# One load of w1 in place of two: the third and fourth column run in packets of 2048 B

## The chip, the core and the metric

The kernel runs on one core of one Trainium2 chip. The metric is the device time of one execution in microseconds. Times in the profile count from the start of the span, the profiled part of one execution.

## The reference

The input is x of 2048 positions by 448 channels in bfloat16. It is normalised (layernorm), and the result xn feeds two branches, whose product is added to x:

```
xn = layernorm(x)
# branch A: a diagonal complex state-space model, 448 states
h[t] = Lam_bar * h[t-1] + B_bar @ xn[t]
s    = 2 * Re(C @ h) + xn * Dskip
# branch B: an MLP, 448 -> 1792 -> 448
y    = layernorm(xn)
g    = silu(gelu(y @ w1 + b1) @ w2 + b2)
out  = x + s * g
```

w1 has 448 rows and 1792 columns, w2 has 1792 rows and 448 columns, both in bfloat16. A row of w1 is 3584 B.

## The kernel before

The 2048 positions are worked in four groups (0 to 3) of 512, each of two blocks of 128 partitions by two positions of different parity. For a group the kernel computes layernorm, transposes the normalised rows (group 0's first layernorm for the MLP by TensorE at L460, the others by DMA on SP), multiplies by w1 (L809), applies gelu (ScalarE, L813), multiplies by w2 (L836), and beside it runs the state-space branch: L737 makes the input of the scan, L761 scans, L879 to L885 make the output.

**The order.** Each operation is added to a plan as a task with the keys that it reads and writes. `ORDER` is a fixed list of task numbers, which is the order of emission on all engines, and `SECOND` is the list of tasks that take their second engine where two are given. Nothing is rearranged when the program is built. From the keys the plan works out the semaphore waits; every DMA has a semaphore of its own. An instruction that waits holds up everything behind it on its engine.

**w1 in SBUF.** w1 has 448 = 384 + 64 rows. The first 384 rows lie as three row blocks of 128 partitions (slots 0 to 2 of `w1_sb`), the last 64 rows on partitions 64 to 127 of slot 3. The matmul of L809 works with halves of 64 partitions at a time, so two of the eight 64-row pieces have to be on the other half of the partitions than the transfer puts them; for one of them a copy inside SBUF (L354, on VectorE) does this: from partitions 64 to 127 of slot 2 to partitions 0 to 63 of slot 3.

**Runs of columns.** The 14 column tiles of 128 are grouped in four runs, `CH` of L344: run 0 has tiles 0 and 1, run 1 tiles 2 to 5, run 2 tiles 6 to 9, run 3 tiles 10 to 13. `ldw1` (L347) loads the runs that it is given: one transfer of 384 rows, one of 64 rows, and then a copy for each run. A row of runs 1 to 3 has 512 columns, 1024 B; a run 0 row has 512 B.

```
CH = ((0, 2), (2, 4), (6, 4), (10, 4))
def ldw1(cs, prio):
    a, w = CH[cs[0]][0] * 128, sum(CH[c][1] for c in cs) * 128
    ld("sp", w1_sb[:, 0:3, a:a + w], ..., [f"w1_{c}" for c in cs], 384 * w * 2, prio, dur=0.55)
    ld("sp", w1_sb[64:128, 3, a:a + w], ..., [f"w1r_{c}" for c in cs], 64 * w * 2, prio)
    for c in cs:
        ...  # the copy within SBUF of run c: reads w1_{c}, writes w1c_{c}
```

**Who waits for w1.** In `mm1_run` (L792) the matmuls of two column tiles come in two phases. The first phase (6 matmuls) waits for both transfers of its run (`w1_c`, `w1r_c`); the second (8 matmuls) waits for the copy too (`w1c_c`). After them comes gelu on ScalarE, which frees the two PSUM banks. In group 0 the pieces are taken up in this order on TensorE: runs 1 and 0 for block 0, then block 1's transposes (L460), then run 2 for block 0, then run 3 for both blocks together, the first matmuls 512 wide; the rest of block 1 follows.

**SP's queue.** SP issues nearly all transfers, in this order: x of blocks 0 and 1, w1 run 1, run 0, run 2, run 3 (two transfers each), x of blocks 2 and 3, w2 in four parts, then B and C of the state-space branch, and from 19.86 us on the DMA transposes.

**VectorE's order around 10 us.** L453 (the layernorm of block 1), L354 (copy of run 2), two L632 (a table of angles), two L419 (block 1's transposes from PSUM to `xn2T`), L354 (copy of run 3), L561, L632, then L401 (statistics of group 1's layernorm).

Of the kernel before, what the change touches and what calls it, by code (L numbers as in the profile page):

```python
# [155 lines left out]
def dram_ap(t, offset, ap):  # L156
    return bass.AP(tensor=t.tensor, offset=offset, ap=ap)
# [2 lines left out]


ORDER = [int(k) for k in """
1 14 20 0 48 10 17 19 21 15 2 95 27 18 96 92 28 93 22 16 25 49 5 97 13 109 94 91 110 98 105 104 26 106 100 23 99 50 51 56 6 52 66 107 3 111 101 112 57
30 108 29 31 102 113 53 115 24 55 33 54 132 58 118 129 32 119 114 122 171 116 34 47 133 169 134 130 40 131 35 67 172 254 251 103 120 156 41 124 252
253 256 255 170 59 117 121 123 4 9 173 44 127 42 125 128 135 141 257 137 126 136 143 60 138 61 258 139 11 142 43 68 144 162 140 148 146 147 176 163 63
8 72 152 39 38 145 205 158 149 151 207 65 36 165 206 154 166 37 259 177 260 164 277 150 155 261 263 62 264 153 262 70 278 179 175 265 168 279 64 174
178 272 273 274 218 71 73 7 283 193 167 191 45 180 217 194 181 182 75 69 275 192 284 76 195 183 276 280 196 287 215 197 199 281 216 285 160 74 184 291
289 288 282 46 198 286 208 85 187 200 209 250 295 210 211 292 89 201 77 78 86 80 203 249 219 204 214 223 224 227 185 202 213 228 231 221 222 188 225
190 226 229 370 79 81 83 266 82 84 290 294 296 293 300 298 230 304 297 87 299 305 212 374 159 368 367 303 301 324 88 302 306 90 325 232 326 307 220
269 270 327 372 271 308 233 186 234 334 472 267 371 369 373 328 268 235 237 238 335 341 342 339 346 343 329 236 312 239 157 340 330 309 382 375 12 241  # L170
331 383 379 384 365 242 245 376 377 332 380 333 336 240 385 243 386 347 348 189 344 316 337 345 387 350 244 338 247 388 361 313 246 310 349 362 389
356 366 352 363 161 320 311 353 364 471 248 314 381 357 358 351 391 359 378 410 414 412 411 360 447 404 473 476 413 418 354 390 419 392 415 416 317
474 475 393 355 417 477 423 421 422 420 394 427 315 478 450 479 397 424 426 395 428 431 432 425 396 400 401 318 448 321 429 434 435 436 430 433 453
451 398 480 406 439 319 449 399 469 483 402 457 440 484 405 407 441 452 408 454 442 409 510 443 481 482 486 470 511 437 512 513 487 489 403 438 505
514 455 485 444 515 490 518 445 494 516 502 322 519 456 517 488 495 520 523 521 446 461 497 506 538 503 539 522 498 507 540 496 541 543 524 542 462
323 544 545 546 491 492 548 547 549 550 552 551 493 499 458 525 526 508 533 534 504 463 464 527 528 535 536 500 554 532 555 557 529 465 459 556 537
572 553 596 460 466 573 574 467 597 599 530 531 575 598 600 601 602 603 576 558 577 580 581 604 509 605 501 582 560 586 561 578 579 563 566 585 607
588 468 583 564 559 592 590 584 606 587 589 591 569 593 594 595 617 562 565 608 614 609 610 611 570 571 567 618 619 612 615 620 616 621 568 622 613
630 623 631 624 632 625 633 626 627 628 629
""".split()]  # L180
SECOND = [int(k) for k in """
46 54 55 62 64 67 70 75 77 84 108 113 131 134 159 161 163 164 166 178 185 186 188 190 191 221 223 225 227 229 231 239 249 250 259 267 269 332 363 365
366 385 401 402 437 448 469 481 483 488 492 500 502 503 505 511 529 530 610 613
""".split()]


# [14 lines left out]
def bass_recurrent_scan__ssm_conv_s5__mixer_channel_mlp__prompt_kernel(  # L201
# [18 lines left out]
    with ExitStack() as es:  # L220
# [85 lines left out]
        with nc.Block():  # L306
# [26 lines left out]
            def ld(eng, o, i, writes, nbytes, prio, reads=(), dur=0.45):  # L333
                kb.dma(eng, o, i, reads=reads, writes=writes, prio=prio, nbytes=nbytes, dur=dur)
# [4 lines left out]
            def ldx(b0, n, prio, reads=(), eng="sp"):  # L339
                ld(eng, x_all[:, b0:b0 + n, :, :], dram_ap(A_x, b0 * 256 * D, [[2 * D, 128], [256 * D, n], [D, 2], [1, D]]),  # L340
                   [f"x{b}" for b in range(b0, b0 + n)], n * 256 * D * 2, prio, reads, dur=0.25 + 0.2 * n)
# [5 lines left out]
            def ldw1(cs, prio):  # L347
                a, w = CH[cs[0]][0] * 128, sum(CH[c][1] for c in cs) * 128
                ld("sp", w1_sb[:, 0:3, a:a + w], dram_ap(B_w1, a, [[F, 128], [128 * F, 3], [1, w]]), [f"w1_{c}" for c in cs], 384 * w * 2, prio, dur=0.55)
                ld("sp", w1_sb[64:128, 3, a:a + w], dram_ap(B_w1, 384 * F + a, [[F, 64], [1, w]]), [f"w1r_{c}" for c in cs], 64 * w * 2, prio)  # L350
                for c in cs:
                    a, w = CH[c][0] * 128, CH[c][1] * 128
                    low, high = w1_sb[0:64, 3, a:a + w], w1_sb[64:128, 2, a:a + w]
                    kb.either(("dve", lambda e, low=low, high=high: e.tensor_copy(low, high)), ("act", lambda e, low=low, high=high: e.activation(low, high, ACT.Copy)), [f"w1_{c}"], [f"w1c_{c}"])  # L354

            LW = ((0,), (1,), (2,), (3,))

            S1 = 10 * PINNED
            for par in range(0 if 0 else 2):
# [1 line left out]
            ldx(1, 1, S1 + 2)  # L361
            ldw1(LW[0], S1 + 1)
            ld("pool", brows[0:3, :], dram_ap(B_b1, 256, [[512, 3], [1, 512]]), ["br0"], 3072, 0, reads=["br"])
            ld("pool", brows[3:4, 0:256], dram_ap(B_b1, 0, [[256, 1], [1, 256]]), ["br1"], 512, 0, reads=["br"])
            for cs in LW[1:]:
                ldw1(cs, S1 + 3)
# [662 lines left out]
```

## Time and profile before

| | |
|---|---|
| median of 3 runs | 153.82 us (153.58 to 154.24) |
| profiled execution | 153.63 us |
| its span | 151.9 us |
| TensorE, matmuls | 147.6 us busy (97%) |
| VectorE | 128.2 us busy (84%) |
| ScalarE | 98.4 us busy (65%) |
| GpSimd | 40.8 us busy (27%) |
| DMA | 14.73 MB, 31236 packets |

The page of the profile names engines by short names: PE is TensorE, PEld its weight loads, DVE VectorE, ACT ScalarE, POOL GpSimd, SP SyncE. An engine with a q behind its name is the queue of that engine. A row of a timeline has the start, the length, the engine, the line of the kernel, the operation, what it writes and reads, the count, and in brackets the idle time before it with what ended it. The tiles of w1 and w2 are both shown as `w_sb`, the rows of normalised x as `xn_sb`.

### The profile page before, as it was taken

What the parts mean: (1) busy time and instruction counts of PE and PEld (TensorE: products, weight loads), DVE (VectorE), ACT (ScalarE), POOL (GpSimd) and SP (SyncE); (2) the same over time, 40 slices, a digit from 0 to 9 for tenths busy, and PEclk for the clock granted to TensorE, in tenths of its full rate; (3) what the DMA queues carried; (4) which work ended last, traced back from release to release, by engine and by line L of the source; (5) the groups of instructions that cost most, each with busy time, mean ns of one, the idle gap of its engine ahead of it and who ended that gap; (6) DMA issues with size and microseconds to landing.
All of it is one profiled execution on the core that took longest, in us unless ns stands there. A gap on an engine that the chain in (4) does not pass through costs nothing.

```text
span 151.9 us, 2990 instructions
## 1 busy us (share of the span) xinstructions
PE 147.6 (97%) x1136; PEld 87.5 (58%) x1136; DVE 128.2 (84%) x270; ACT 98.4 (65%) x182; POOL 40.8 (27%) x100
## 2 busy tenths in 40 slices
PE   7999999999999999999999999999999999999992
PEld 7886755444566577545444556754444666555561
DVE  3978969899998969999999996379968727999984
ACT  3787998888789559997798610462579833067400
POOL 5377870053021910010366006200071040000200
PEclk9999999999999999999999999999999999999999
DMA  4999999889996100700003032610340001100022
GB/s 117 270 309 389 262 231 182 175 150 154 214 213 165 23 0 0 138 0 4 0 0 63 4 60 53 146 60 4 60 109 14 4 0 60 60 0 0 4 102 79
DMA packets 31236, 14.73 MB, mean 97 GB/s; under 512 B 24752, under 2 KB 30774, under 8 KB 31222
## 3 DMA queue, kind: packets, MB, share of 16 engines
q1 hardware_dynamic: 30912, 14.26, 41.9%
q0 software_dynamic: 160, 0.23, 0.6%
q8 instruction: 9, 0.15, 0.4%
q10 hardware_dynamic: 150, 0.05, 0.1%
q14 instruction: 5, 0.04, 0.1%
HBM read 6.89 MB, written 1.84 MB: 57 GB/s over the span
## 4 chain that ended last, share of the span: by engine, by line
PE 96%; DVE 2%; issue 0%; DVEq 0%
PE psum L809 29%; PE psum L836 28%; PE psum L737 14%; PE psum L879 12%; PE psum L882 4%; PE psum L422 3%; PE psum L720 3%; PE psum L885 1%; DVE t L893 1%; PE psum L460 1%; DVE tmp L899 1%; PE psum L705 1%; PE psum L602 0%; DVE ones L309 0%; PE psum L529 0%
## 5 line engine op out<-in xcount | busy, mean ns | idle before, releaser
L809 PE MATMUL psum<-xn2T,w_sb 64*128 64x512 bf16 (+1 forms) x462 | 44.6, 345 | 0.2
L836 PE MATMUL psum<-w_sb,gT 128*128 128x448 bf16 x224 | 44.4, 353 | 0.0
L813 ACT ACTIVATE gT<-psum,b1f 128x512 bf16<-128x512 f32 (+1 forms) x66 | 36.0, 625 | 10.6 <-PE psum L809 10.4
L809 PEld LDWEIGHTS psum<-xn2T,w_sb 64*128 64x128 bf16 x462 | 24.0, 109 | 19.7 <-ACT gT L813 2.3
L836 PEld LDWEIGHTS psum<-w_sb,gT 128*128 128x128 bf16 x224 | 21.6, 98 | 20.3 <-issue 0.6
L419 ACT ACTIVATE u_sb<-psum 128x512 bf16<-128x512 f32 (+2 forms) x22 | 10.5, 478 | 23.0 <-PE psum L737 22.7
L737 PE MATMUL psum<-xnT,BT 128*128 128x256 bf16 x196 | 24.0, 273 | 0.0
L737 PEld LDWEIGHTS psum<-xnT,BT 128*128 128x128 bf16 x196 | 18.9, 98 | 5.4 <-issue 1.1
L761 DVE TENSOR_TENSOR_SCAN s_w<-dk,vs 128x774 f32<-128x774 f32 x8 | 14.0, 1760 | 0.1
L899 POOL TENSOR_TENSOR tmp<-t,x_all 128x448 bf16<-128x448 bf16 x5 | 5.2, 1031 | 33.1 <-DVE t L896 30.7
L500 ACT ACTIVATE xn_sb<-x_all,lnw 128x448 bf16<-128x448 bf16 (+2 forms) x21 | 13.0, 661 | 1.2 <-DVE xn_sb L499 1.1
L419 ACT ACTIVATE vs<-s_w 64x256 bf16<-64x256 f32 (+2 forms) x16 | 10.9, 682 | 2.6 <-DVE s_w L761 1.5
L879 PE MATMUL psum<-CZ,h_sb 128*128 128x448 bf16 x56 | 11.9, 353 | 0.0
L839 DVE TENSOR_TENSOR o<-psum,b2bc 128x448 f32<-128x448 f32 x16 | 9.7, 614 | 1.7 <-PE psum L836 1.5
L879 PE MATMUL psum<-CQ,h_sb 128*128 128x448 bf16 (+2 forms) x54 | 10.5, 332 | 0.0
L879 PEld LDWEIGHTS psum<-CZ,h_sb 128*128 128x128 bf16 x56 | 5.4, 98 | 4.7 <-DVE lnmv L407 0.4
L401 DVE BATCH_NORM_STATS2 lnst<-x_all 128x6 f32<-128x448 bf16 x12 | 7.0, 614 | 0.6 <-DMA x_all<-in_A_x_dram 0.6
L879 PEld LDWEIGHTS psum<-CQ,h_sb 128*128 128x128 bf16 x54 | 5.1, 98 | 4.0 <-DVE t L893 0.4
L882 PE MATMUL psum<-M,xnT 128*128 128x448 bf16 x32 | 7.4, 352 | 0.0
L891 DVE TENSOR_TENSOR Cr<-psum,xd 128x448 f32<-128x448 f32 x7 | 4.3, 620 | 3.5 <-PE psum L885 3.4
L480 POOL TENSOR_TENSOR lnw<-lnw,mhalf 128x8 f32<-128x8 f32 x3 | 7.0, 2332 | 0.3
L499 DVE TENSOR_SCALAR xn_sb<-x_all,lnw 128x448 bf16<-128x448 bf16 (+2 forms) x19 | 6.9, 395 | 0.0
(160 smaller groups left out, 189.8 us busy)
## 6 DMA issues: line engine op xcount, KB each, us to landing
out_dram<-tmp SPq DMA_DIRECT2D x7, 224.0 KB, 2.0
x_all<-in_A_x_dram SPq DMA_DIRECT2D x3, 448.0 KB, 4.3
w_sb<-in_B_w_dram SPq DMA_DIRECT2D x3, 448.0 KB, 8.5
w_sb<-in_B_w_dram SPq DMA_DIRECT2D x3, 384.0 KB, 4.9
vs<-in_A_C_re_dram SPq DMA_DIRECT2D x1, 392.0 KB, 11.5
Bn<-in_A_B_im_dram SPq DMA_DIRECT2D x1, 336.0 KB, 10.4
Bn<-in_A_B_re_dram SPq DMA_DIRECT2D x1, 336.0 KB, 10.8
vs<-in_A_C_im_dram SPq DMA_DIRECT2D x1, 336.0 KB, 11.3
```

Source lines behind the costliest of these rows:

```text
L401: dve([lambda e, b=b, par=par, q=q: e.bn_stats(lnst[:, q, :], x_all[:, 2 * g + b, par, :])], [f"x{2 * g + b}"] , [f"st{q}"], 0.62, prio)
L419: kb.either(("act", [lambda e, o=o, i=i: e.activation(o, i, ACT.Copy) for o, i in pairs]), ("dve", [lambda e, o=o, i=i: e.tensor_copy(o, i ...
L480: power = fns + [lambda e: e.tensor_tensor(w(2), w(0), mhalf[:].to_broadcast([128, 2, nq]), ALU.pow), lambda e: e.tensor_tensor(w(3), mean ...
L500: ("act", [lambda e, o=o, i=i: e.activation(o, i, ACT.Identity, bias=nb, scale=rs) for o, i in parts], 0.75, 0.2)]
L737: fns = [lambda e, r=r, m=m, d=d: e.matmul(psum[:, 4, r * NK:(r + 1) * NK], BT[:, m, d, :], xnT[:, gx, d, :], start=(d == 0), stop=(d == 6 ...
L761: dve(lambda e, so=so, vi=vi: e.tensor_tensor_scan(so, dk[:].rearrange("p i c -> p (i c)"), vi, 0.0, ALU.mult, ALU.add), ["v", "vl", "dk", ...
L809: return lambda e: e.matmul(view(bk[k]), w1_sb[rows, d, fcol(2 * j + k)], rhs[rows, d, :, :], start=not second and n == 0, stop=second and ...
L813: act([lambda e, k=k: e.activation(gT[:, gb, 2 * j + k, :].rearrange("p (r c) -> p r c", r=2)[:, :, cols], view(bk[k]), ACT.Gelu_apprx_tan ...
L836: fns = [lambda e, fi=fi: e.matmul(psum[:, bk, 0:D], gT[:, gb, fi, q * 128:(q + 1) * 128], w2_sb[:, fi, :], start=(fi == 0), stop=(fi == N ...
L839: dve(lambda e: e.tensor_tensor(o2[:, fb, :], psum[:, bk, 0:D], b2bc[:], ALU.add), [f"ps{bk}", "b2bc"], [f"oo{fb}"], 0.62, prio - 76)
L879: fns = [lambda e, k=k: e.matmul(psum[:, bk, c0:c1], h_sb[:, hb, k, k0:k0 + 128], cm[:, k, c0:c1], start=(k == 0), stop=False) for k in ra ...
L882: fns += [lambda e, d=d: e.matmul(psum[:, bk, c0:c1], xnT[:, gx, d, xs], M0[:, d, c0:c1], start=False, stop=(d == 3)) for d in range(4)]
```

## The change

Runs 2 and 3 go to `ldw1` in one call. There is then one transfer of 384 rows by 1024 columns (768 KB) and one of 64 rows by 1024 columns (128 KB), where there were two transfers of 384 KB and two of 64 KB. A row of it is 2048 B in place of 1024 B. The two copies within SBUF stay as they are; both now depend on the transfer of 384 rows. The tasks have new numbers because there are two fewer, so `ORDER` and `SECOND` are renumbered; the order of all other tasks is as before. SP's queue holds the two new transfers where the first two of the four were.

```diff
-            LW = ((0,), (1,), (2,), (3,))
+            LW = ((0,), (1,), (2, 3))
...
             ldw1(LW[0], S1 + 1)
...
             for cs in LW[1:]:
                 ldw1(cs, S1 + 3)
```

## The prediction

> **What bounds the kernel now.** I read the page first: busy times, then the slices, then the chain of waits.
>
> ```profile
> PE 147.6 (97%) x1136; PEld 87.5 (58%) x1136; DVE 128.2 (84%) x270; ACT 98.4 (65%) x182; POOL 40.8 (27%) x100
> PEclk9999999999999999999999999999999999999999
> DMA  4999999889996100700003032610340001100022
> PE 96%; DVE 2%; issue 0%; DVEq 0%
> ```
>
> TensorE is busy for 97% of the span and 96% of the chain that ended last is its matmuls, one after the other, at a granted clock near full throughout. So the end of the kernel moves by what TensorE is held up, almost one for one, and by nothing else. The DMA engines are full from about 4 to 46 us (a slice is 3.8 us; the first four to six slices hold the loads). The change touches only loads of w1, so the question is whether TensorE comes to wait for one of them.
>
> The timelines of TensorE, of its weight loads and of VectorE around 10 us show where w1 is taken up:
>
> ```profile
> 9.58 0.62 PE L460 MATMUL psum<-ident,xn_sb 128*128 128x128 bf16 x8
> 10.14 1.51 PE L809 MATMUL psum<-xn2T,w_sb 64*128 64x256 bf16 x22
> ```
>
> ```profile
> 10.13 0.25 PEld L809 LDWEIGHTS psum<-xn2T,w_sb 64*128 64x128 bf16 x6
> 10.58 1.35 PEld L809 LDWEIGHTS psum<-xn2T,w_sb 64*128 64x128 bf16 x26 [0.20 <-ACT gT L813]
> ```
>
> ```profile
> 9.31 0.31 DVE L354 COPY w_sb<-w_sb 64x512 bf16<-64x512 bf16 x1 [0.88 <-DMA w_sb<-in_B_w_dram]
> 9.66 0.62 DVE L632 TENSOR_SCALAR s_w<-dk,cw 128x256 f32<-128x256 f32 x2
> 10.19 0.75 DVE L419 COPY xn2T<-psum 128x512 bf16<-128x512 bf16 x2
> 10.97 0.29 DVE L354 COPY w_sb<-w_sb 64x512 bf16<-64x512 bf16 x1
> 12.15 0.63 DVE L401 BATCH_NORM_STATS2 lnst<-x_all 128x6 f32<-128x448 bf16 x1 [0.44 <-DMA x_all<-in_A_x_dram]
> ```
>
> The matmuls at 10.14 are the first that read run 2 of w1 (the program's third run, columns of tiles 6 to 9). They wait for both its transfers, the 384 rows and the 64 rows. VectorE's copy at 9.31 waits for the 384 rows alone, and its idle time of 0.88 us ends with that landing. The queue of transfers says when each landed (answers for windows that hold one issue; KB, then us from issue to landing; issues begin at 4.44, 5.07, 5.61 and 6.24):
>
> ```profile
> w_sb<-in_B_w_dram SPq DMA_DIRECT2D x1, 384.0 KB, 4.9
> w_sb<-in_B_w_dram SPq DMA_DIRECT2D x1, 64.0 KB, 4.5
> w_sb<-in_B_w_dram SPq DMA_DIRECT2D x1, 384.0 KB, 5.2
> w_sb<-in_B_w_dram SPq DMA_DIRECT2D x1, 64.0 KB, 4.8
> ```
>
> So run 2 is complete at 5.07 + 4.46 = 9.53 (the 384 rows at 9.29), and run 3 at 6.24 + 4.78 = 11.02 (its 384 rows at 10.77). TensorE needs run 2 at 10.14, 0.6 us after it lands, and run 3 only with the first 512-wide matmul, at 11.81, 0.8 us after. Both are covered today, by little.
>
> **The change, part by part.** Compared instruction by instruction, every engine but SP keeps its order; SP's four issues become two, in the same place. So the change does what it says; what else can move is time.
>
> 1. *The wait that it adds.* Run 2 no longer lands by itself: everything that wants run 2 waits for run 3 too. At the present rate the last 64 rows would be in at 11.02 as now, since the queue holds the same bytes behind the same predecessors and the DMA engines are full (next table).
>
> 2. *The packets.* 896 packets of 1024 B become 448 of 2048 B. No row has this size, so I bound its rate by the stretches around it (columns: stretch, length, busy of PE, PEld, DVE, ACT, POOL, clock, DMA share, GB/s):
>
> ```profile
> 6.90:8.60 1.70, 1.65 (x32) 1.53 (x33) 1.48 (x8) 1.55 (x3) 0.39 (x1) 1.00 0.98 315
> 8.60:10.10 1.50, 1.50 (x28) 1.22 (x24) 0.76 (x3) 1.25 (x4) 1.21 (x3) 1.00 1.05 270
> 10.10:11.60 1.50, 1.50 (x27) 1.27 (x27) 1.44 (x6) 1.18 (x5) 1.33 (x3) 1.00 1.01 330
> 11.60:12.30 0.70, 0.70 (x14) 0.45 (x9) 0.26 (x2) 0.70 (x2) 0.62 (x3) 1.00 1.02 369
> 12.30:13.50 1.20, 1.20 (x18) 0.66 (x16) 1.20 (x3) 0.95 (x4) 0.54 (x4) 1.00 1.00 387
> ```
>
> Runs 2 and 3 hold 917,504 B and fill the engines from 6.9 to about 10.1; (1.70 x 315 + 1.50 x 270) / 3.2 = 294 GB/s, or 3.12 us. After 10.1 come x, in packets of 1792 B, and w2, mostly in packets of 3584 B. At 330 GB/s the two runs take 2.78 us, 0.34 less; at 369, 0.63 less; at 387, 0.75 less; at the present rate nothing less. I take 330: the stretch after 10.1 is the one nearest in packet size that is not mostly 3584 B. The ends are 0 and 0.75. A loss below zero I keep for a rival. The last rows then land at 11.02 - 0.34 = 10.68, between 10.27 and 11.02. That last landing is the slowest of the DMA engines, and I leave its lag behind the mean as it is.
>
> 3. *TensorE.* The copy at 9.31 began 0.02 after its landing, so the matmuls of 10.14 would begin at 10.70: 0.56 later. Of that, 0.10 is given back at once: the next run of matmuls started at 10.59 because it waited for ScalarE's gelu (the 0.20 of the weight loads above), while its predecessors, at 0.11 us a pair, would have let it go at 10.49. Net +0.46, between 0.05 and 0.80. After that ScalarE's gelu waits for matmuls and the matmuls for gelu, both shifted alike; I find no stretch of TensorE idle time up to 147 us that a DMA or another unshifted thing ends, so the 0.46 reaches the end.
>
> 4. *VectorE behind the added wait.* The first L354 copy waits for the merged 384 rows. They lose the 64 rows that went between (0.24 in landing) and gain most of the 0.34: 10.77 - 0.24 - 0.3 = 10.2. Queued behind it are two L632 (0.62), the two L419 that move block 1's transposes into xn2T, and the other L354. They move by 0.94, so xn2T is ready at 10.94 + 0.94 = 11.9. The 512-wide matmuls need it at 11.81 + 0.46 = 12.27: covered by 0.4. The margin holds if the merged load is later still, since the matmuls wait for the 64 rows behind it. The second copy ends at 12.2 and is needed a microsecond later still. Then L401 is 0.94 - 0.44 = 0.5 late, and with it the layernorm of group 1 and its DMA transposes on SP (issued 19.86 and 21.87, landing 5.4 us later, 27.3; wanted at 30.0). VectorE's next wait for TensorE, 1.20 us before L839 at 22.26, takes up the rest. Cost: nothing, with 0.4 and over 2 us of cover.
>
> 5. *SP.* Two issues fewer (0.50 and 0.59 us, with gaps 1.17): x, w2 and the rest are issued 1.17 earlier. In a full queue this moves their landing only by the 0.3 saved. w2 lands last at 18.5 against 19.3 when it is wanted. Gain: nothing. GpSimd's load of b2, which waits for run 3's 64 rows, is issued at 13.58, long after them.
>
> Sum: +0.46. The profiled execution took 153.63 us (span 151.9, and 1.7 around it), 0.19 under the median of 153.82; the median moves to 154.28, say 154.3. About 0.5%, 0.77 us, is what a measurement of this kernel can tell from no change; the forecast lies inside that.
>
> **Rivals.** *Larger transfer, free of charge* (10%): if packets of 2048 B run like those of 3584 B, at 387 GB/s and more, 0.75 to 0.9 us is saved, the rows are in by 10.1 to 10.3, and TensorE is held by 0.05 or nothing: 153.8 to 153.9. For it: the rate rises steadily in the table. Against it: from 6.9 to 10.1 packets also suffer long latencies that are not a matter of size. The Trainium skill, "DMA: Bandwidth & Descriptors", sections "Anatomy of one DMA" and "Bandwidth", speaks for this rival: it fits a load as 2.0 us plus bytes over 436 GB/s (for GpSimd's queue) and advises batching to 1 MiB. By that, an estimate, the 768 KB would land 3.8 us after issue, at 8.2, and cost nothing; but it gives 2.9 us for the 384 KB that took 4.9 here, so the trace does not bear it out in a full queue.
>
> *The slowest engine decides* (35%): a merged load is complete when the last DMA engine is. Net cost passes 0.77 if the start of the matmuls passes 11.01, which is when the last rows land no earlier than they do now. This happens if the larger packets bring no rate, or if an engine lags. For it: w2's first load, issued at 7.41, took 6.8 us, to 14.2, while x before it was in by 12.2, though its 224 KB need 0.6 us at 369 GB/s: 1.4 us of lag; a fetch of instructions (16 KB) sat on an engine just then. Today such a lag under run 3 has 0.8 us of cover, and after the change none. Price: no rate gained, 154.6; with 1.0 us of lag, 10.68 + 1.0, start at 11.70, net +1.46, 155.3. Against it: the stretch before 10 us shows no such fetch.
>
> *Faster* (7%): the earlier issue pulls in something that TensorE waits for. The trace lists 1.6 us of idle time before weight loads from 9.5 to 20, but ended by ScalarE, by TensorE itself or by issue, not by a DMA. It would give 153.0 at best.
>
> **How the numbers follow.** The forecast, a net cost from 0.1 to 0.77, has 48%. Same: forecast 48% and the free transfer 10%, 58%. Slower: 35%. Faster: 7%. The range goes from 153.6 (the free transfer, less the scatter of the runs before) to 155.1 (a lag of 0.8 us) and leaves out the faster case and the largest lags.
>
> **What would show it.** Right: L809's matmuls of run 2 begin at 10.5 to 11.0 instead of 10.14, with TensorE idle behind the L460 transposes; VectorE's idle time before L354 grows from 0.88 to about 1.9; the later pieces of the chain are shifted by one constant. Wrong: no idle time there (free transfer), matmuls after 11.0 (slowest engine), a second new wait at the 512-wide matmuls for xn2T, or a shift that is not constant after 20 us.

## The result and the profile after

The changed kernel takes 154.93 us in the median (154.83 to 155.79), the kernel before 153.82. The ratio is 1.0088, with a 95% interval of 1.006 to 1.0116: slower by about 1.4 us by the ratio, 1.1 by the medians. The ratios, here and below, leave out slow runs, those that took over 1.5% longer than the fastest of the same kernel; f1_after, f2_join and f4_alone have such runs. The forecast of 154.3, inside the bound of 0.5%, was wrong; the rival of the slowest DMA engine, with 154.6 to 155.3, was right. The stated range, up to 155.1, still holds the 154.93, but on that rival's side of the bound.

The execution whose trace is kept took 155.79 us, one of the two longest. Its span is 2.1 us longer than the one of before, so sizes read from it stand above those of a median run. The page's lines for TensorE, the clock, the DMA engines and the chain of waits:

```profile
PE 147.9 (96%) x1136; PEld 88.0 (57%) x1136; DVE 127.9 (83%) x270; ACT 98.4 (64%) x182; POOL 40.3 (26%) x100
PEclk9999999999999999999999999999999999999999
DMA  4999999989996300510003030801322001200022
PE 89%; DMA 5%; SPq 2%; DVE 1%; issue 1%; DVEq 0%
```

TensorE has the same work (147.9 us against 147.6), but the chain now runs through a load: 7.18 us of it, from 4.42 to 11.60, is the transfer of w1. The timelines of TensorE, its weight loads and VectorE at the same place as before:

```profile
9.95 0.62 PE L460 MATMUL psum<-ident,xn_sb 128*128 128x128 bf16 x8
12.32 2.95 PE L809 MATMUL psum<-xn2T,w_sb 64*128 64x256 bf16 x42 [1.75 <-DMA w_sb<-in_B_w_dram]
```

```profile
12.29 1.94 PEld L809 LDWEIGHTS psum<-xn2T,w_sb 64*128 64x128 bf16 x34 [1.89 <-DMA w_sb<-in_B_w_dram]
```

```profile
11.62 0.29 DVE L354 COPY w_sb<-w_sb 64x512 bf16<-64x512 bf16 x1 [2.81 <-DMA w_sb<-in_B_w_dram]
11.94 0.62 DVE L632 TENSOR_SCALAR s_w<-dk,cw 128x256 f32<-128x256 f32 x2
12.48 0.74 DVE L419 COPY xn2T<-psum 128x512 bf16<-128x512 bf16 x2
13.25 0.29 DVE L354 COPY w_sb<-w_sb 64x512 bf16<-64x512 bf16 x1
```

Run 2's matmuls begin at 12.32 instead of 10.14, after 1.75 us of idle time that the load ends. No 0.20 us of waiting for ScalarE follows. From there every piece of the chain is shifted by one constant: the first product with w2 from 19.39 to 21.46 (2.07), the last output matmuls from 145.43 to 147.51 (2.08). The landings (issued at 4.42 and 5.04):

```profile
w_sb<-in_B_w_dram SPq DMA_DIRECT2D x1, 768.0 KB, 7.2
w_sb<-in_B_w_dram SPq DMA_DIRECT2D x1, 128.0 KB, 7.2
```

The last 64 rows are in at 12.23 (5.04 + 7.19), where run 3's were in at 11.02. A landing is the last of 16 marks, one by each DMA engine. The fastest engine finished the 64 rows at 9.22, before at 9.54; the slowest is 3.0 us behind it, before 1.5.

### The profile page after: what moved, and what is told of

Its sections match the earlier page's. It is cut to its first block, busy times and chain, and to the rows that moved or that the text cites. A ratio compares the mean times of both kernels' runs of the same rounds, so it can differ in the third digit from the quotient of the medians.

```text
span 154.0 us, 2987 instructions
## 1 busy us (share of the span) xinstructions
PE 147.9 (96%) x1136; PEld 88.0 (57%) x1136; DVE 127.9 (83%) x270; ACT 98.4 (64%) x182; POOL 40.3 (26%) x100
## 4 chain that ended last, share of the span: by engine, by line
PE 89%; DMA 5%; SPq 2%; DVE 1%; issue 1%; DVEq 0%
PE psum L836 28%; PE psum L809 27%; PE psum L737 14%; PE psum L879 12%; DMA w_sb<-in_B_w_dram 5%; PE psum L882 4%; PE psum L720 3%; SPq L84 2%; PE psum L885 1%; DVE t L893 1%; DVE tmp L899 1%; PE psum L705 1%; DVEq L138 0%
## 5 line engine op out<-in xcount | busy, mean ns | idle before, releaser
L809 PE MATMUL psum<-xn2T,w_sb 64*128 64x512 bf16 (+1 forms) x462 | 44.5, 345 | 1.9 <-DMA w_sb<-in_B_w_dram 1.7
L809 PEld LDWEIGHTS psum<-xn2T,w_sb 64*128 64x128 bf16 x462 | 24.1, 109 | 21.3 <-ACT gT L813 2.1
L419 ACT ACTIVATE u_sb<-psum 128x512 bf16<-128x512 f32 (+2 forms) x22 | 10.5, 478 | 23.0 <-PE psum L737 22.7
L879 PE MATMUL psum<-CQ,h_sb 128*128 128x448 bf16 (+2 forms) x54 | 10.5, 332 | 0.0
```

What stands on the lines that cost most here:

```text
L419: kb.either(("act", [lambda e, o=o, i=i: e.activation(o, i, ACT.Copy) for o, i in pairs]), ("dve", [lambda e, o=o, i=i: e.tensor_copy(o, i ...
L809: return lambda e: e.matmul(view(bk[k]), w1_sb[rows, d, fcol(2 * j + k)], rhs[rows, d, :, :], start=not second and n == 0, stop=second and ...
L879: fns = [lambda e, k=k: e.matmul(psum[:, bk, c0:c1], h_sb[:, hb, k, k0:k0 + 128], cm[:, k, c0:c1], start=(k == 0), stop=False) for k in ra ...
```

## The experiments

The theories: A, the added wait is the cost, and packets of 2048 B make it longer because the slowest engine lands later; B, the added wait alone; C, something else than this wait; D and E, the size of the transfer or the earlier issue of x. F, G and H came up on the way and are told with their experiments. Most experiments have a kernel with one of these taken out. The figures of each are ratios to the kernel before, run on the same chip.

**e1_join and f2_join: the wait without the packets.** One kernel, run on two chips.

```diff
+        for t in self.tasks:          # run 2's users wait for run 3's transfers
+            if "w1_2" in t.reads:
+                t.deps.add(self.tasks[33])
+                if t.eng == "pe":
+                    t.deps.add(self.tasks[34])
```

> The four transfers of before, in packets of 1024 B and in their old places, but everything that wants run 2 also waits for run 3's transfers, as after the change. Theory A (the added wait is the cost, and packets of 2048 B make its landing worse): last rows at about 11.0 as in before, run 2's matmuls at 11.05 instead of 10.14, net +0.8 us: 154.6, less than the 1.1 of the changed kernel. Theory B (the added wait alone, packets do not matter): as the changed kernel, +1.1 us, 154.9. Theory C (something other than this wait): within 0.3 us of before.

> As e1_join: four transfers in packets of 1024 B, run 2's users wait for run 3 as well. Theory A: +0.6 to +0.7 us, last rows at about 11.05. Theory B: as f1_after.

Measured: 1.0042 (1.0025 to 1.0059), 0.65 us; and 1.0061 (1.0036 to 1.0086), 0.94 us. The last rows land at 11.05 and 10.96, as before the change. TensorE's rows of f2_join:

```profile
9.88 0.62 PE L465 MATMUL psum<-ident,xn_sb 128*128 128x128 bf16 x8
11.09 0.63 PE L814 MATMUL psum<-xn2T,w_sb 64*128 64x256 bf16 x8 [0.60 <-DMA w_sb<-in_B_w_dram]
```

(L814 is L809 there.) So the wait alone costs 0.65 to 0.94 us, around the 0.80 that the prediction had for "no rate gained": about half to two thirds of the loss needs no larger packet.

**f1_after: the changed kernel beside f2_join.**

> The changed kernel once more, on the same chip as the three that follow. Theory A (the added wait, and packets of 2048 B that land later at the slowest DMA engine than packets of 1024 B): +1.0 to +1.3 us, last 64 rows of w1 between 11.3 and 12.2, so 0.3 to 0.6 us more than f2_join. Theory B (the wait alone; the difference between the two seen so far was the chip's or chance): the same as f2_join within 0.2 us.

Measured: 1.0089 (1.0068 to 1.0111), 1.4 us; the last rows at 11.96, the matmuls at 12.05. The difference of the two ratios is 0.0028, 0.4 us, but the intervals overlap (to 1.0086, and from 1.0068). The first pair, the seven runs of the result and e1_join, differs by 0.0046, 0.7 us, with intervals that just miss each other (from 1.006, and to 1.0059). By time alone theory A is likely and not shown; the landings, below, bear it out.

**e4_noneed: the loads without the wait.**

```diff
-   ... w1_sb[rows, d, fcol(2 * j + k)] ...
+   ... w1_sb[rows, d, fcol(2 * j + k if g or c < 2 else 2 + k)] ...
+   r = c if g else min(c, 1)         # keys w1_r, w1r_r, w1c_r in place of c
... # in ORDER, task 32 (copy of run 2) is moved to just before task 33
```

> The changed kernel's loads, but nothing early waits for them: group 0's matmuls of the column tiles of runs 2 and 3 read run 1's weights instead (this part of the result is left out), and VectorE's copy of run 2 stands behind the two L419. Theories A, B, D and E, in all of which the price is paid through this wait: 153.8, within 0.3 us of before. Theory C (the cost arises elsewhere, for instance in later loads or in SP's queue): +0.8 us or more stays.

Measured: 0.9992 (0.9975 to 1.001). TensorE goes on behind the transposes without a gap, while the last rows land at 11.32:

```profile
9.23 0.62 PE L461 MATMUL psum<-ident,xn_sb 128*128 128x128 bf16 x8
9.78 2.48 PE L811 MATMUL psum<-xn2T,w_sb 64*128 64x256 bf16 x34
```

The whole price is paid at this wait; theory C falls. Later loads, two issues fewer on SP and the earlier x neither cost nor gain anything that can be measured.

**e2_rows: packets of 2048 B in smaller transfers.**

```diff
+   ld("sp", w1_sb[:, 0, 768:1792], dram_ap(B_w1, 768, [[F, 128], [1, 1024]]), ...)
+   ld("sp", w1_sb[:, 1, 768:1792], dram_ap(B_w1, 128 * F + 768, [[F, 128], [1, 1024]]), ...)
+   ld("sp", w1_sb[:, 2, 768:1792], dram_ap(B_w1, 256 * F + 768, [[F, 128], [1, 1024]]), ...)
+   ld("sp", w1_sb[64:128, 3, 768:1792], dram_ap(B_w1, 384 * F + 768, [[F, 64], [1, 1024]]), ...)
... # and all users of runs 2 and 3 wait for these four
```

> Runs 2 and 3 together in packets of 2048 B as after the change, but in four transfers, by rows: 128, 128, 128 and 64; all their users wait for all four (the copies for the third), and x is issued as late as in before. Theory A (packet size): as the changed kernel, +0.9 to +1.3 us, about 154.9, last rows near 11.3 to 12.2. Theory D (one large transfer is what makes an engine lag, or x issued 1.17 us earlier crowds it): last rows at about 11.0 or before, +0.5 to +0.8 us.

Measured: 1.0049 (1.0029 to 1.0068), 0.75 us, with runs from 153.84 to 155.32. By time this lies in theory D's range, and its interval overlaps those of the changed kernel (from 1.006) and of both joined runs: inconclusive. The last rows of the kept trace land at 11.79, like those of the one large transfer. That trace is of the longest of the twelve runs; for a median run, 0.46 us shorter, 11.3 is an estimate.

**e3_latex: x issued late.**

```diff
+        self.tasks[45].deps.add(self.tasks[55])     # x of blocks 2, 3 waits for L541
```

> The changed kernel, with the load of x for blocks 2 and 3, and so all of SP's queue behind it, held back to about 6.9 us by a wait for ScalarE's activation at L541, as late as in before. Theory E (x and w2, issued earlier, crowd the merged load and make its last engine late): last rows at 10.6 to 11.0, +0.5 to +0.8 us. Theories A and D: as the changed kernel, +1.1 us, 154.9.

x was issued at 6.55, and the last rows of w1 still landed at 12.08: theory E falls. The time was not what any theory said: 1.0132 (1.0082 to 1.0182), with three runs at 154.94 to 155.27 and three at 157.1. In those three the mean granted clock is 0.989. Stretches of the kept trace, one of the three (columns as in the prediction; the clock is the number before the last two):

```profile
9.90:12.10 2.20, 0.05 (x1) 0.00 (x0) 0.60 (x3) 1.10 (x4) 1.95 (x5) 0.99 1.02 291
12.10:14.00 1.90, 1.83 (x18) 1.56 (x20) 1.84 (x8) 0.00 (x0) 1.16 (x5) 0.50 1.04 397
14.00:16.00 2.00, 2.00 (x22) 1.34 (x19) 2.00 (x6) 1.46 (x4) 0.15 (x1) 0.63 1.07 395
16.00:18.00 2.00, 2.00 (x26) 1.38 (x24) 1.97 (x9) 0.95 (x4) 1.40 (x3) 1.00 1.10 269
```

TensorE waits from 9.95 to 12.17, and just as its matmuls begin the clock is halved, for 3.4 us. The wait then costs about 2 us more. The changed kernel is exposed to it too: one of f1_after's six runs has a mean clock of 0.988 and took 157.62; none of the seven first runs did. So is the wait alone: one of f2_join's twelve runs has a mean clock of 0.989 and took 156.77. No trace of these two runs was kept. No run of the kernel before whose clock is on record has a mean under 0.997.

**f3_warm: the wait filled.**

```diff
...
+   + [lambda e: e.matmul(psum[:, 6, 256:384], ones[:, :], ones[:, :], start=True, stop=True)
+      for _ in range(24 if b and not par else 0)]       # added to e3_latex
```

> e3_latex with 24 idle-filling matmuls of 128 columns on TensorE behind block 1's transposes, into an unused part of a PSUM bank (about 1.3 us of the wait). Theory F (e3_latex's runs at 157.1 us lost TensorE's clock because TensorE sat idle for over 2 us): no run with a mean granted clock under 0.995, all runs between 154.8 and 155.4. If the clock is lost for another reason, about half of the runs are again at 157.

Measured: 1.0094 (1.0075 to 1.0114), six runs from 154.95 to 155.56, none with a mean clock under 0.997, and the last rows at 12.03. Two of the six lie above the 155.4 that was expected, by 0.1 to 0.2 us. The idle time before run 2's matmuls is 0.71 us in its trace, against 2.21 in e3_latex. This fits theory F. Six runs are few for an event that took three of six in e3_latex and one of six in f1_after, so that the filling prevents it is likely and not settled.

**f4_alone, g2_alone2k_again, g1_alone1k, g3_alone1k_again: w1 without x beside it.** x and all loads behind it are held until w1 is in, once with the changed kernel's loads (the first two), once with f2_join's (the others).

```diff
+        self.tasks[45].deps.add(self.tasks[31])     # f4, g2; in g1, g3 tasks 47 and 34
```

> The changed kernel, with x of blocks 2 and 3 and all of SP's queue behind it issued only when the last rows of w1 have landed; only the landing of w1 is of interest, since the later loads are late. Theory G (in the changed kernel the fast DMA engines go on to x while the slow ones are still at w1, and their traffic makes the slow ones later): last rows at 10.2 to 10.8. Theory A without crowding (the packets themselves): 11.3 to 12.2 as in the changed kernel.

> f4_alone once more, for a second landing of the packets of 2048 B without x beside them. Theories A and H: 10.7 to 11.2, as the first time. If it lands at 11.3 to 12.2, the first landing was chance and x's traffic plays no part.

> f2_join (four transfers, packets of 1024 B, joined waits), with x of blocks 2 and 3 and all of SP's queue behind it issued only when run 3's last rows have landed; only the landing of w1 is of interest. Theory A (the packets of 2048 B are by themselves slower to the last engine): last rows at 10.0 to 10.5, at least 0.5 us before the 11.01 that packets of 2048 B took under the same hold. Theory H (the size only matters through the traffic of x that overlaps it): 10.8 to 11.1, as with 2048 B.

> g1_alone1k once more, for a second landing. Theory A: 10.0 to 10.5. Theory H: 10.8 to 11.1.

The kernels' own times (155.1 to 161.4 us) say nothing here, since all later loads are late. The landings of w1's last 64 rows in every kept trace, with the mean over the 16 engines and the mean time of one packet of w1 from about 5.9 us on (marks and packets as the trace records them):

| kernel | packet | x beside it | last engine, us | mean engine, us | mean packet, ns |
|---|---|---|---|---|---|
| before | 1024 B | yes | 11.02 | 10.21 | 57 |
| e1_join | 1024 B | yes | 11.05 | 10.43 | 61 |
| f2_join | 1024 B | yes | 10.96 | 10.18 | 57 |
| g1_alone1k | 1024 B | no | 10.86 | 10.19 | 57 |
| g3_alone1k_again | 1024 B | no | 10.71 | 10.18 | 58 |
| after | 2048 B | yes | 12.23 | 10.46 | 116 |
| e2_rows | 2048 B | yes | 11.79 | 10.26 | 111 |
| e3_latex | 2048 B | later | 12.08 | 10.83 | 120 |
| e4_noneed | 2048 B | yes | 11.32 | 10.50 | 113 |
| f1_after | 2048 B | yes | 11.96 | 10.52 | 118 |
| f3_warm | 2048 B | later | 12.03 | 10.12 | 105 |
| f4_alone | 2048 B | no | 11.00 | 10.03 | 107 |
| g2_alone2k_again | 2048 B | no | 12.03 | 10.66 | 125 |

With x beside it, the last engine is in at 10.96 to 11.05 with packets of 1024 B (three traces) and at 11.32 to 12.23 with 2048 B (six, two of them with x issued later), one execution each: this bears theory A out. e2_rows, with transfers of 128 rows, lies with the larger packets, which speaks against D; but it is one trace, and its time lies in D's range, so D is not excluded. Holding x back brings packets of 1024 B forward by 0.2 us, so they missed the 10.0 to 10.5 that theory A had expected, and g1_alone1k's 10.86 lies where theory H had it. f4_alone's 11.00 looked as if x were the cause for 2048 B, g2_alone2k_again's 12.03 took that back. The mean engine, from 10.03 to 10.83 with 2048 B and from 10.18 to 10.43 with 1024 B, is not earlier with the larger packets.

## Why the prediction was wrong

*Step 2, the packets, is the step that failed.* It took 330 GB/s for packets of 2048 B, a gain of 0.34 us, and left the slowest engine's lag behind the mean as it was. Both terms were wrong. A packet of 2048 B takes 105 to 125 ns in the mean against 57 to 61 for 1024 B, so in the mean nothing is gained per byte: for one of the 16 engines, 28 packets at 116 ns (changed kernel) are 3.2 us, and so are 56 at 57 ns (before). The median packet is better, 84 ns against two of 46, but long packets eat it up: the longest of the two runs took 1.27 us in the changed kernel and 0.73 before (over all kept traces 0.57 to 1.59 us with 2048 B, 0.58 to 1.05 with 1024 B). The rates of the stretches after 10 us, from which the term was read, belong to other transfers at another time. And the lag of the last engine behind the mean grew from 0.6 to 0.8 us (1024 B with x beside it) to 0.8 to 1.9 us (2048 B). With x beside them, the last rows came at 11.3 to 12.2 instead of 10.68. Of the loss of 1.1 to 1.4 us, the wait alone makes 0.65 to 0.94, and the packets the rest.

*Why the lag grows* was not tried further. The traces do not name the engine that moved a packet. An engine has half as many packets, and a slow packet holds up twice the bytes; that is an argument, not a result. The Trainium skill, "DMA: Bandwidth & Descriptors", section "Latency and other measured facts", gives 0.2 us for an HBM access on average and 2 us at high load; packets of up to 1.27 us beside a median of 84 ns would fit such a spread, but no run here measures a single access or shows where a packet's time goes.

*Step 1, the added wait,* was right in kind and in its bound: with no rate gained, 0.80 net, and e1_join and f2_join gave 0.65 and 0.94.

*Step 3, TensorE,* was right: start of run 2's matmuls, 0.10 given back, then a constant shift. In the kept trace 12.32 - 10.14 = 2.18, less 0.10, is 2.08, and the chain's end moved by 2.08. For a median run, 1.1 us more, it gives a start at 11.34, an estimate. What it left out is the clock: in e3_latex a wait of 2.21 us came with half the clock for 3.4 us, and this was no term of the sum. In the seven runs of the result, with mean clocks from 0.998, it played no part.

*Step 4, VectorE,* was right to cost nothing: its idle time grew from 0.88 to 2.81 (1.9 foretold), and xn2T is ready at 13.22; with run 2 at 12.32 the first 512-wide matmul is due at 14.0. *Step 5, SP,* also: e4_noneed stays at the time of before.

*The rivals.* The slowest engine, given 35%, had mechanism, place and price: no gain in rate and a lag, from 154.6 to 155.3. The example on which it leaned, an engine held up by a fetch of instructions, was not needed: the changed kernel's trace has no packet of 16 KB from 4 to 15 us. The free transfer fell: in that trace a packet of 2048 B takes 116 ns in the mean, and one of w2's 3584 B, up to 15 us, 148 ns, a good quarter less per byte. The Trainium skill, "DMA: Bandwidth & Descriptors", section "Anatomy of one DMA", would have had the 768 KB in 3.8 us, an estimate by its fit for GpSimd's queue; in the seven traces with that transfer they took 6.2 to 7.3.

No version here beats the kernel before: with the wait taken out (e4_noneed) its time is reached, not passed, since before the change no load was waited for on TensorE.

## What to carry to other kernels

When two loads are joined, ask which consumer of the first now waits for the second, and what cover it had: here 0.6 us of cover turned into a wait, and that alone cost 0.65 to 0.94. A load lands when the slowest of 16 engines does, so a mean rate, and the rate of another transfer at another time above all, is no forecast of a landing; keep the lag of the last engine as a term of its own with its own range. Here larger packets improved the median packet, and what counted was the slowest engine. A wait on TensorE can cost more than its own length, when the clock is halved behind it: about 2 us more in e3_latex.

## What the runs showed of the hardware

Packets of 2048 B from HBM brought no higher mean rate than packets of 1024 B in a full queue (105 to 125 ns against 57 to 61), and a later last engine (11.32 to 12.23 against 10.96 to 11.05 us with x beside them).

TensorE lost its clock in a wait of 2.21 us in e3_latex: it went from 1.00 to 0.50 at 12.07 us, for 3.41 us. Two other runs of the six have the same mean clock of 0.989, the other three do not. g2_alone2k_again shows the same in its later wait for w2, from 21.26 to 24.24, where the clock was halved at 23.34 for 6.83 us:

```profile
21.30:23.30 2.00, 0.00 (x0) 0.00 (x0) 1.80 (x10) 2.00 (x6) 0.00 (x0) 1.00 1.09 326
23.40:26.70 3.30, 2.46 (x7) 1.02 (x8) 1.92 (x9) 2.19 (x4) 1.04 (x4) 0.50 1.17 215
26.80:30.10 3.30, 3.30 (x10) 1.32 (x9) 0.36 (x1) 0.00 (x0) 0.44 (x3) 0.50 1.74 150
30.20:32.00 1.80, 1.80 (x11) 0.95 (x10) 1.77 (x5) 1.22 (x2) 0.00 (x0) 1.00 0.66 124
```

The traces show when this happens. In each kept trace the moments at which the clock changes lie whole multiples of 3.413 us apart: 2, 1 and 41 of them in e3_latex, 5, 2 and 38 in g2_alone2k_again, 43 or 44 in the others. Take each stretch of 3.413 us on that grid, within the span, which ran at the full clock, and the share of it in which TensorE has matmuls or transposes. In the five stretches at whose end the clock was halved, the share is 16 to 38% (38% in e3_latex, 37% in g2_alone2k_again, the others at the kernel's end). In all those behind which the clock stayed full it is 49% or more: 49% in the changed kernel's trace, 57% in f1_after, 63% in e2_rows. Where between 38 and 49% the border lies, no run here shows. The grid lies differently in every run, so one wait can keep or lose the clock by chance: e2_rows waited 2.06 us, but 0.79 of it fell into one stretch and 1.27 into the next, and the clock stayed.

The Trainium skill, "TensorE: Matmul & The Clock Gate", section "Part 1: The HAM clock gate", describes a window of about 3.4 us that runs freely, so that the moment of a change depends on where in it the work begins, and half the clock after an idle window. The length of the stretches and the part of chance agree. That the window has to be idle does not: in e3_latex TensorE was busy for 38% of it.
